# Batch 2's transposes moved to DMA, one in-place ring, and a new front order in a fused attention and FFN kernel

## The chip, the cores and the metric

One core of one Trainium2 chip. Kernels are compared only within the same rounds. The metric is device time in microseconds (us) of one execution. Single executions of one kernel differ by up to 3 us, so a profile (one execution) is used to say *where* time goes, and ratios over several runs say *how much*.

## The reference

```python
# q, k, v: (8 batches, 12 heads, 448 positions, 64)
scores = scale * np.matmul(q, k.transpose(0, 1, 3, 2))
attn = np.maximum(scores, 0.0) ** 2 / S
x = np.matmul(attn, v)                 # -> (3584 tokens, 768)
h = x @ w_in                           # 768 -> 2048
g = 0.5 * h * (1.0 + erf(h / sqrt(2))) # exact GELU
out = g @ w_out                        # 2048 -> 768
```

## The kernel before

Python builds the whole instruction order with a small list scheduler: every piece of work is an `Op` with estimated times, and each engine takes the ready op with the smallest key. The chip runs that fixed order. For batches from 2 on, TensorE's order is given: "slots" of attention with "atoms" of FFN mixed in. Below, QK is the product of q and k, AV that of the squared scores and v, and xT the AV result, which two copies bring from PSUM to SBUF. The first weights are `w_in`, the second weights `w_out`, and second products the matmuls with them. An FFN group is 6 matmuls 448 wide, or 12 of 224. Eviction is the work of VectorE and ScalarE that empties PSUM.

```python
WINDOW = 60                  # only the first 60 open ops of an engine are looked at
def pick(self, ops):
    ...
        key = (est + op.bias + (0.5 * dur if len(op.engines) > 1 else 0), n)
```

Transposes of q and k: batches 0 to 2 on TensorE with a PSUM copy, batches 3 to 7 by a VectorE permute and a DMA transpose on SP. `add_gate` makes GpSimd, which issues the loads, wait for the q transposes before its next load.

```python
def add_tk(b, g):            # TensorE
    ...                      # 14 nc.tensor.transpose into one PSUM tile "tp"
    op = sch.add((("PE", 0.45, 0.67),), fn, ld_k[b, g], need=("f",), mode="T", bias=T_BIAS)
    ev = sch.add(e_copy(2 * S, 2), fn2, [op] + old_T(b), frees=("f",))

def add_T_dma(b, after):     # SP: 3 of kT, then 4 of qT
    ...
        nc.sync.dma_start_transpose(get_T(b)[1][:, g]..., get_p()[1][:, g])

# attention: score -> relu (ACT, early also DVE) -> square (DVE) -> AV
box["ar"] = apool.tile([128, 2, S], BF16, tag="ar", name="a_relu")         # ring of 3
box["a2"] = apool.tile([128, 2, S], BF16, tag="a2", name="a_sq", bufs=NA)  # ring of 11
...
# order of the loads on GpSimd and of the early work
add_v(0, 0, 1)
for g in (1, 2):
    add_k(0, g, g + 1); add_q(0, g, g + 1, 0, HC); add_v(0, g, g + 1)
add_win(0); add_q(0, 0, G, HC, NC); add_win(1)
...                          # transposes and steps of batch 0, loads of batch 1 and 2
add_wout(0); add_wout(1)     # second weights, straight after batch 2's loads
add_steps(steps(1), dve=True)
for g in range(G):
    add_tk(2, g); add_tq(2, g)
...
    if b == 2:
        stage.append(x1[:8] + mix(x1[8:], x2))   # x1: FFN-in of batch 1, x2: FFN-out of batch 0
```

Of the kernel before, what the change touches and what calls it, by code (L numbers as in the profile page):

```python
# [9 lines left out]
BF16 = mybir.dt.bfloat16  # L10
# [6 lines left out]
HS = S // 2  # L17
KB = 64
NK = S // KB
NA = 11  # L20
HP = H // 2
G = H // 4
DM = H * D
# [3 lines left out]
ND = DM // 2  # L27
NB = 512
WINS = (2, 2, 4, 4, 4)
T_BIAS, AV_BIAS, F1_BIAS, GELU_BIAS = -0.3, 0.0, 0.2, -0.4  # L30


def cols(half):
# [7 lines left out]
class Op:  # L41
# [1 line left out]



    def __init__(self, engines, fn, deps=(), need=(), frees=(), bias=0.0, mode=None, joint=()):
        self.engines, self.fn, self.deps = engines, fn, list(deps)
        self.need, self.frees, self.bias, self.mode = need, frees, bias, mode
        self.joint = joint
        self.done = None  # L50


class Scheduler:



    SWITCH = 0.09
    COLD = 18.0
    WINDOW = 60

    def __init__(self, buffers):
        self.free = {"PE": 0.6, "ACT": 2.2, "DVE": 1.0, "POOL": 1.25, "SP": 0.9}
        self.bufs = {name: [0.0] * n for name, n in buffers.items()}
        self.open, self.mode, self.dma = [], None, 2.6
        self.landed = [0.0] * 8
        self.log = []

# [18 lines left out]
    def pick(self, ops):  # L86
        top = None
        for n, op in enumerate(ops):
            t = self.ready(op)
            if t is None:  # L90
                continue
            for eng, dur, lat in op.engines:
                est = max(t, self.free[eng])
                if isinstance(lat, tuple):
                    est = max(est, self.landed[-8])
                if eng == "PE" and op.mode != self.mode:
                    est += self.SWITCH
                key = (est + op.bias + (0.5 * dur if len(op.engines) > 1 else 0), n)
                if top is None or key < top[0]:
                    top = (key, est, op, eng, dur, lat)  # L100
        return top

    def commit(self, est, op, eng, dur, lat):
        if eng == "PE":
            self.mode = op.mode
            if est < self.COLD:
                dur, lat = 2 * dur, 2 * lat
        if isinstance(lat, tuple):
            t = max(self.dma, est + dur + 1.0)
            self.dma = t + lat[0] / (300e3 if t < 10 else 390e3)  # L110
            op.done = self.dma + 1.2
            self.landed += [op.done] * lat[1]
        else:
            op.done = est + lat
        self.free[eng] = est + dur
        for name in op.need:
            b = self.bufs[name]
            b[b.index(min(b))] = math.inf
        ends = [op.done] + [o.done for o in op.joint]
        if None not in ends:  # L120
            for name in op.frees:
                b = self.bufs[name]
                b[b.index(math.inf)] = max(ends)
        self.log.append((est, op, eng))
# [32 lines left out]
def kernel(  # L157
# [23 lines left out]
    tpool = pool("tpool", 2)  # L181
    xpool = pool("xpool", 2)
    hpool = pool("hpool", 2)
    apool = pool("apool", 3)
    opool = pool("opool", 3)
    w_pp = pool("w_pp", 3, PS)
    f_pp = pool("f_pp", 2, PS)
# [77 lines left out]
        d = 0.07 + n / psum / 960  # L265
        return ("DVE", d, d + 0.12), ("ACT", 0.12 + 0.00074 * n, 0.24 + 0.00074 * n)

    sch = Scheduler({"w": 3, "ar": 3, "a2": NA, "f": 2, "osb": 3})
    pool_q, pe_q = [], []

    def dma(fn, nbytes, deps=(), issues=1):
# [70 lines left out]
        for e in range(2):  # L342
            copy(dst[e], src[:, 2 * e : 2 * e + 2].rearrange("p j (c d) -> p j c d", d=D))  # L343

    def add_pk(b, g0, g1, after=()):
        for g in range(g0, g1):
            deps = ld_k[b, g] + [Tk[max(b - 1, 1), x][0] for x in range(G)] + list(after)
            Pk[b, g] = sch.add(
                (("DVE", 0.31, 0.43),),
                lambda e, g=g: permute_k(V.tensor_copy, g, nk[b][:, 2 * g : 2 * g + 2]), deps,  # L350
            )

    def add_pq(b, g0, g1, c0=0, c1=NC, after=()):
        for g in range(g0, g1):
            deps = [ld_q[b, g, c] for c in range(c0, c1)] + list(after)
            deps += [Tq[max(b - 1, 1), g, c][0] for c in range(c0, c1)]
            if b == 3:
                deps += [Tq[1, x, c][0] for x in range(G) for c in range(NC)]
            d = 2 * (0.07 + (c1 - c0) * 128 / 3840)

            def fn(e, g=g):
                permute_q(
                    V.tensor_copy, g, c0, c1, nq[b][:, 4 * g : 4 * g + 4, c0 * D : c1 * D]
                )

            op = sch.add((("DVE", d, d + 0.12),), fn, deps)
            for c in range(c0, c1):
                Pq[b, g, c] = op

    def old_T(b):  # L370
        return [o for (bb, *_), o in QK.items() if bb == b - 2]

    def add_tk(b, g):
        box = []

        def fn(e):
            tp = f_pp.tile([128, NK * 128], BF16, tag="f", name="tp")
            box.append(tp)
            for i in range(NK):
                for e in range(2):  # L380
                    nc.tensor.transpose(  # L381
                        tp[64 * e : 64 * e + 64, bass.ts(i, 128)],
                        nk[b][:, 2 * g + e, bass.ts(i, D)],
                        ident,
                    )

        def fn2(e):
            copy(e, get_T(b)[1][:, g], box[0])

        op = sch.add(  # L390
            (("PE", 0.45, 0.67),), fn, ld_k[b, g], need=("f",), mode="T", bias=T_BIAS
        )
        ev = sch.add(e_copy(2 * S, 2), fn2, [op] + old_T(b), frees=("f",))
        Tk[b, g] = (op, ev)
        return op

    def add_tq(b, g, c0=0, c1=NC):
        box, n = [], (c1 - c0) * KC

        def fn(e):  # L400
# [11 lines left out]
        def fn2(e):  # L412
            copy(e, get_T(b)[0][:, 2 * g : 2 * g + 2, c0 * KC : c1 * KC], box[0])

        d = 0.125 * (c1 - c0)
        deps = [ld_q[b, g, c] for c in range(c0, c1)]
        op = sch.add(
            (("PE", d, d + 0.22),), fn, deps, need=("f",), mode="T", bias=T_BIAS
        )
        ev = sch.add(e_copy(2 * n, 2), fn2, [op] + old_T(b), frees=("f",))  # L420
        for c in range(c0, c1):
            Tq[b, g, c] = (op, ev)
        return op
# [38 lines left out]
    def add_steps(todo, bias=0.0, dve=False):  # L462
        for blocks in todo:
# [17 lines left out]
                            )  # L481

            def fn_relu(e_, box=box, used=used):
                box["ar"] = apool.tile([128, 2, S], BF16, tag="ar", name="a_relu")
                ar, ps = box["ar"][:, :, :used], box["ps"][:, :, :used]
                if e_ == "ACT":
                    A.activation(ar, ps, AF.Relu, scale=c_att)  # L487
                else:
                    V.tensor_scalar(  # L489
                        ar, ps, c_att, 0.0,  # L490
                        op0=mybir.AluOpType.mult, op1=mybir.AluOpType.max,
                    )

            def fn_mul(e_, box=box, used=used):
                box["a2"] = apool.tile([128, 2, S], BF16, tag="a2", name="a_sq", bufs=NA)
                ar = box["ar"][:, :, :used]
                V.tensor_mul(box["a2"][:, :, :used], ar, ar)  # L497

            deps = []
# [7 lines left out]
            if dve:  # L507
                d = 0.07 + 2 * used / 960
                eng += (("DVE", d, d + 0.12),)
            o2 = sch.add(eng, fn_relu, [o1], need=("ar",), frees=("w",))  # L510
            d = 0.07 + used / 960
            o3 = sch.add((("DVE", d, d + 0.12),), fn_mul, [o2], need=("a2",), frees=("ar",))
            for x, blk in enumerate(blocks):
                QK[blk] = o1
                SQ[blk] = (o3, box, x * w)
# [4 lines left out]
    def add_av(blk, bias):  # L520
# [5 lines left out]
        def fn(e_):  # L526
# [19 lines left out]
        d = 7 * 0.19 * w / S  # L546
        op = sch.add(
            (("PE", d, d + 0.24),), fn, deps, mode="A", bias=bias + AV_BIAS, need=("w",),
            frees=("a2",) * gone,
        )  # L550
        AV[b, g, half] = op

# [7 lines left out]
        for j in range(2):  # L560
            xs.append(
                sch.add(
                    e_copy(w, 1), lambda e, j=j: copy(e, get_x()[:, j], pav[0][:, j, :w]),
                    [op] + old, frees=("w",), joint=list(xs),
                )
            )
        xs[0].joint = [xs[1]]
# [157 lines left out]
    ctx.enter_context(tc.manual_schedule())  # L725


    add_v(0, 0, 1)
    for g in (1, 2):
        add_k(0, g, g + 1)  # L730
        add_q(0, g, g + 1, 0, HC)
        add_v(0, g, g + 1)
    add_win(0)
    add_q(0, 0, G, HC, NC)
    add_win(1)
# [22 lines left out]
        add_tk(0, g)  # L758
        add_tq(0, g, 0, HC)
    for g in range(G):  # L760
        add_tq(0, g, HC, NC)
    add_steps(halves(0), dve=True)
    add_load(1, 0, 1)
    add_win(2)
    add_load(1, 1, 2)
# [1 line left out]
    add_load(1, 2, 3)  # L767
    add_win(4)
    for g in range(G):
        add_tk(1, g)  # L770
        add_tq(1, g)
    for m in range(0, KF, 2):
        add_f1(0, m, 0, bias=F1_BIAS)
    for g in range(G):
        add_load(2, g, g + 1)
    add_wout(0)
    add_wout(1)
    add_steps(steps(1), dve=True)
    for g in range(G):
        add_tk(2, g)  # L780
        add_tq(2, g)
    for m in range(0, KF, 2):
        add_f1(0, m, 1, bias=F1_BIAS)


    todo = [x for b in range(2, B) for x in steps(b)]
# [19 lines left out]
    for b in range(2, B):  # L806
        add_steps(steps(b))
        if b + 1 < B:

            n = per * (b - 2) + {2: 4, 3: 3}.get(b, 1)  # L810
            add_pk(b + 1, 0, G, after=at(n))
            add_pq(b + 1, 0, G, after=at(n))
            add_T_dma(b + 1, [at(n + (y >= 4)) for y in range(7)])
# [2 lines left out]
                add_load(b + 2)  # L816
        x1, x2 = f1(b - 1), f2(b - 2)
        if b == 2:
            stage.append(x1[:8] + mix(x1[8:], x2))
        else:  # L820
            stage.append(x2[:2] + mix(x1, x2[2:]))
    for n, slot in enumerate(order):
        for kind, x in slot:
            pe_q.append(AV[x] if kind == "AV" else QK[x])
# [39 lines left out]
```

## Time and profile before

| | before |
|---|---|
| median of 4 runs | 404.26 us (403.62 to 404.96) |
| span of the profiled run | 401.4 us, granted clock 0.996 |
| TensorE from first transpose to first FFN matmul ("front") | 6.14 to 24.64 us |
| from there to the first QK of batch 2 ("middle") | 24.64 to 64.25 us |
| from there on ("body") | 332 us, idle 0.36 us |

The lines behind the table are in the prediction. The page's shares say "TensorE, 97%", but that is an average: the body has one limit, and the front and middle have several (rows arriving, eviction of scores, order). A gain has to be looked for ahead of 64 us.

### The profile page before, as it was taken

To read this page: it belongs to the slowest core of one execution; us is meant where nothing else is said; L and a number is where in the kernel's file an instruction comes from. 1 tells how busy PE (TensorE), PEld (TensorE's weight loads), DVE (VectorE), ACT (ScalarE), POOL (GpSimd) and SP (SyncE) were. 2 spreads that over 40 slices of the span, in tenths; PEclk is the share of its full clock that TensorE was granted. 3 is DMA by queue.
4 is the path that set the end of the run, shared out by engine and by line. 5 is a ranking of instruction groups with operands and counts; after the bars stand their busy time and mean duration, and the time that the engine had idled before them with its cause. 6 is when DMAs were issued, how large, how long until landed. Compare 5 with 4: busy or idle time off the path is not lost.

```text
span 401.4 us, 8294 instructions
## 1 busy us (share of the span) xinstructions
PE 387.8 (97%) x3587; PEld 218.7 (54%) x3587; DVE 175.4 (44%) x323; ACT 214.8 (54%) x326; POOL 45.1 (11%) x67
## 2 busy tenths in 40 slices
PE   7699999999999999999999999999999999999995
PEld 6476686555555455555554555555555555555562
DVE  2989951454535434633373443634343433110111
ACT  2887956755746646656645565457645646222200
POOL 8755420000200200020001100000000000000000
PEclk9899999999999999999999999999999999999999
DMA  9999999719975592689137921470102011100132
GB/s 172 192 204 203 201 211 206 111 48 162 169 126 109 93 214 50 126 120 179 41 65 153 179 67 42 88 129 1 41 13 66 3 41 40 41 17 24 39 80 78
DMA packets 63750, 41.59 MB, mean 104 GB/s; under 512 B 32097, under 2 KB 60129, under 8 KB 63713
## 3 DMA queue, kind: packets, MB, share of 16 engines
q0 software_dynamic: 30496, 22.47, 37.3%
q1 hardware_dynamic: 32944, 18.13, 20.1%
q8 instruction: 28, 0.46, 0.5%
q10 hardware_dynamic: 272, 0.46, 0.3%
q14 instruction: 10, 0.07, 0.1%
HBM read 45.61 MB, written 11.01 MB: 141 GB/s over the span
## 4 chain that ended last, share of the span: by engine, by line
PE 86%; DVE 6%; DMA 3%; issue 2%; POOL 1%; ACT 0%; POOLq 0%
PE pso L621 36%; PE psh L581 36%; PE pav L534 7%; PE ps L475 7%; DVE a_sq L497 2%; DVE a_relu L489 2%; DMA nk<-in_k_dram 2%; DMA win_sb<-in_moe_w_in_dram 2%; POOL v_sb L307 1%; POOL nq L208 0%; DVE pq L343 0%; POOL nk L292 0%; PE tp L381 0%; DVE kT L259 0%; DVE osb L259 0%
## 5 line engine op out<-in xcount | busy, mean ns | idle before, releaser
L487 ACT ACTIVATE a_relu<-ps 128x896 bf16<-128x896 f32 (+1 forms) x156 | 136.9, 918 | 47.0 <-PE ps L475 45.1
L581 PE MATMUL psh<-xT,win_sb 128*128 128x448 bf16 (+1 forms) x864 | 156.2, 332 | 0.5 <-DVE osb L259 0.4
L621 PE MATMUL pso<-wout_sb,h_sb 128*128 128x384 bf16 x896 | 152.8, 326 | 0.0
L497 DVE TENSOR_TENSOR a_sq<-a_relu 128x896 bf16<-128x896 bf16 (+1 forms) x169 | 102.9, 620 | 81.8 <-ACT a_relu L487 81.8
L621 PEld LDWEIGHTS <-h_sb 128*128 128x128 bf16 x896 | 86.3, 98 | 63.1 <-issue 5.9
L581 PEld LDWEIGHTS <-win_sb 128*128 128x128 bf16 x864 | 80.9, 98 | 68.1 <-issue 13.6
L593 ACT ACTIVATE h_sb<-psh 128x448 bf16<-128x448 f32 x128 | 70.6, 552 | 76.4 <-PE psh L581 76.4
L259 DVE COPY osb<-pso 128x384 f32<-128x384 f32 x56 | 31.1, 556 | 92.7 <-PE pso L621 92.7
L475 PE MATMUL ps<-qT,kT 64*64 64x448 bf16 (+1 forms) x756 | 47.0, 340 | 2.8 <-DVE xT L259 1.4
L534 PE MATMUL pav<-a_sq,v_sb 64*64 64x448 bf16 (+1 forms) x756 | 37.4, 332 | 0.4 <-ACT a_relu L487 0.4
L261 ACT CAST xT<-pav 128x448 bf16<-128x448 f32 (+1 forms) x31 | 14.6, 482 | 33.8 <-PE pav L534 33.8
L475 PEld LDWEIGHTS <-kT 64*64 64x64 bf16 x756 | 19.2, 107 | 21.8 <-issue 15.5
L259 DVE CAST xT<-pav 128x448 bf16<-128x448 f32 (+1 forms) x23 | 13.7, 594 | 39.2 <-ACT xT L261 39.2
L534 PEld LDWEIGHTS <-v_sb 64*64 64x64 bf16 x756 | 19.7, 106 | 15.3 <-issue 7.4
L450 POOL COPY gate<-qT 128x4 bf16<-128x4 bf16 x4 | 0.8, 189 | 154.7 <-DMA qT<-pq 154.7
L489 DVE TENSOR_SCALAR a_relu<-ps 128x896 bf16<-128x896 f32 x13 | 14.1, 1082 | 0.5 <-PE ps L475 0.5
L208 POOL DMA_DIRECT2D nq<-in_q_dram x14 | 11.8, 840 | 2.6 <-PE ps L475 0.9
L307 POOL DMA_DIRECT2D v_sb<-in_v_dram x14 | 10.6, 760 | 2.9 <-DMA win_sb<-in_moe_w_in_dram 1.5
L292 POOL DMA_DIRECT2D nk<-in_k_dram x13 | 9.9, 764 | 8.8 <-PE ps L475 6.0
L381 PE MATMUL tp<-ident,nk 128*64 128x128 bf16 x126 | 5.6, 232 | 2.2 <-DMA nk<-in_k_dram 2.2
L406 PE MATMUL tp<-ident,nq 112*64 112x112 bf16 x144 | 5.9, 223 | 1.8 <-DMA nq<-in_q_dram 1.3
L343 DVE COPY pq<-nq 112x512 bf16<-112x512 bf16 x30 | 6.9, 285 | 0.0
(25 smaller groups left out, 51.9 us busy)
## 6 DMA issues: line engine op xcount, KB each, us to landing
nk<-in_k_dram POOLq DMA_DIRECT2D x5, 672.0 KB, 7.1
nq<-in_q_dram POOLq DMA_DIRECT2D x5, 672.0 KB, 10.7
v_sb<-in_v_dram POOLq DMA_DIRECT2D x5, 672.0 KB, 13.6
wout_sb<-in_moe_w_out_dram POOLq DMA_DIRECT2D x2, 1536.0 KB, 18.4
out_dram<-osb SPq DMA_DIRECT2D x8, 336.0 KB, 2.8
out_dram<-osb SPq DMA_DIRECT2D x8, 288.0 KB, 2.9
v_sb<-in_v_dram POOLq DMA_DIRECT2D x9, 224.0 KB, 8.4
out_dram<-osb SPq DMA_DIRECT2D x8, 240.0 KB, 2.7
```

The lines of the kernel that those rows point to most:

```text
L208: nc.gpsimd.dma_start(nq[b][:, 4 * g0 : 4 * g1, c0 * D : c1 * D], q_view(b, g0, g1, c0, c1))
L259: V.tensor_copy(dst, src)
L261: A.copy(dst, src)
L307: nc.gpsimd.dma_start(vt[b][:, 2 * g0 : 2 * g1], kv_view(v, b, g0, g1))
L475: nc.tensor.matmul(ps[64 * j : 64 * j + 64, e, x * w : x * w + w], kT[r, g, i * 128 + 64 * j : i * 128 + 64 * j + 64], qT[r, 2 * g + j, co ...
L487: A.activation(ar, ps, AF.Relu, scale=c_att)
L489: V.tensor_scalar(ar, ps, c_att, 0.0, op0=mybir.AluOpType.mult, op1=mybir.AluOpType.max,)
L497: V.tensor_mul(box["a2"][:, :, :used], ar, ar)
L534: nc.tensor.matmul(pav[0][o2 : o2 + 64, e, :w], vt[b][r, 2 * g + e, bass.ts(i, D)], box["a2"][r, e, o : o + w], start=(i == 0), stop=(i == ...
L581: nc.tensor.matmul(ph[:, x * n : x * n + n], win_sb[:, kd, bass.ts(m + x, 128)], xT[b][:, kd, c], start=(kd == 0), stop=(kd == KD - 1),)
L593: A.activation(hT[b // 2][:, m : m + nm, o + c.start : o + c.stop], box[0][:, :S].rearrange("p (x n) -> p x n", x=nm), AF.Gelu,)
L621: nc.tensor.matmul(po[:, :ND], hT[pr][:, kf, bass.ts(t, 128)], wout_sb[:, kf, bass.ts(n, ND)], start=(kf == 0), stop=(kf == KF - 1),)
```

## The change

Its intent: take batch 2's transposes off TensorE; put them ahead of the second weights in the load queue, so that the two don't run side by side; let relu and square share one ring; and place work of batch 0's first half in front. The diff, cut to its core, with some lines joined:

```diff
-NA = 11
+NA = 14
+T_BIAS, T_LATE, T_ONE, T_TWO = -0.5, 0.2, -0.16, 0.6    # and eight more biases
+DMA_FREE, DMA_LAT, LEAD = 4.0, 2.13, 5
 ...
-                key = (est + op.bias + (0.5 * dur if len(op.engines) > 1 else 0), n)
+                key = (est + op.bias + x * op.other, n)
 ...
-                box["ar"] = apool.tile([128, 2, S], BF16, tag="ar", name="a_relu")
+                box["a2"] = apool.tile([128, 2, S], BF16, tag="a", name="a_sq")
 ...                                        # the square writes the tile that it reads
-    add_v(0, 0, 1)
     for g in (1, 2):
         add_k(0, g, g + 1)
         add_q(0, g, g + 1, 0, HC)
-        add_v(0, g, g + 1)
+        add_v(0, g - 1, g)
+    add_v(0, 2, 3)
 ...
+        half = [order_only(QK[0, G - 1, NK - 1, 0])]
+        add_tk(1, g, T_ONE, half)          # batch 1's transposes after half 0's scores
+        add_tq(1, g, bias=T_ONE, after=half)
 ...
-    add_wout(0)
-    add_wout(1)
-    add_steps(steps(1), dve=True)
-    for g in range(G):
-        add_tk(2, g)
-        add_tq(2, g)
+    add_steps(steps(1), ATT1_BIAS, True)
+    for g in range(G):
+        add_pk(2, g, g + 1, bias=T_TWO)
+        add_pq(2, g, g + 1, bias=T_TWO)
+    add_T_dma(2, [[]] * 7)
+    add_gate(2)
+    add_wout(0)
+    add_wout(1)
 ...
-            n = per * (b - 2) + {2: 4, 3: 3}.get(b, 1)
+            n = per * (b - 2) + {2: 5, 3: 3}.get(b, 1)
 ...
-            stage.append(x1[:8] + mix(x1[8:], x2))
+            first_atoms = x1[:LEAD]        # ahead of batch 2's first scores
+            stage.append(x1[LEAD:] + x2)
```

More of the change, by code (lines that the diff above doesn't have):

```diff
@@ L29 @@
 WINS = (2, 2, 4, 4, 4)
-T_BIAS, AV_BIAS, F1_BIAS, GELU_BIAS = -0.3, 0.0, 0.2, -0.4
+T_BIAS = -0.5
+T_LATE = 0.2
+T_ONE = -0.16
+T_TWO = 0.6
+AV_BIAS = -0.11
+X_BIAS = -0.2
+F1_BIAS = 0.2
+F1B_BIAS = 0.2
+ATT1_BIAS = 0.0
+HALF_BIAS = -0.07
+GELU_BIAS = -0.57
+RELU_DVE = 0.36
+DMA_FREE = 4.0
+DMA_LAT = 2.13
+SWITCH = 0.09
+LEAD = 5
 def cols(half):
@@ L41, with __init__, done @@
 class Op:
-    def __init__(self, engines, fn, deps=(), need=(), frees=(), bias=0.0, mode=None, joint=()):
+    def __init__(self, engines, fn, deps=(), need=(), frees=(), bias=0.0, mode=None, joint=(),
+                 other=0.0):
         self.engines, self.fn, self.deps = engines, fn, list(deps)
         self.need, self.frees, self.bias, self.mode = need, frees, bias, mode
+        self.other = other
         self.joint = joint
-        self.done = None
+        self.start = self.done = None
+class order_only:
+    def __init__(self, op):
+        self.op = op
+    @property
+    def done(self):
+        return self.op.start
 class Scheduler:
-    SWITCH = 0.09
     COLD = 18.0
@@ L63, in __init__ @@
         self.bufs = {name: [0.0] * n for name, n in buffers.items()}
-        self.open, self.mode, self.dma = [], None, 2.6
+        self.open, self.mode, self.dma = [], None, DMA_FREE
         self.landed = [0.0] * 8
@@ L91, in pick @@
                 continue
-            for eng, dur, lat in op.engines:
+            for x, (eng, dur, lat) in enumerate(op.engines):
                 est = max(t, self.free[eng])
@@ L96, in pick @@
                 if eng == "PE" and op.mode != self.mode:
-                    est += self.SWITCH
-                key = (est + op.bias + (0.5 * dur if len(op.engines) > 1 else 0), n)
+                    est += SWITCH
+                key = (est + op.bias + x * op.other, n)
                 if top is None or key < top[0]:
@@ L103, in commit @@
     def commit(self, est, op, eng, dur, lat):
+        op.start = est
         if eng == "PE":
@@ L109, in commit @@
             t = max(self.dma, est + dur + 1.0)
-            self.dma = t + lat[0] / (300e3 if t < 10 else 390e3)
-            op.done = self.dma + 1.2
+            self.dma = t + lat[0] / 390e3
+            op.done = self.dma + DMA_LAT
             self.landed += [op.done] * lat[1]
@@ L183 @@
     hpool = pool("hpool", 2)
-    apool = pool("apool", 3)
+    apool = pool("apool", NA)
     opool = pool("opool", 3)
@@ L266, in e_copy @@
         return ("DVE", d, d + 0.12), ("ACT", 0.12 + 0.00074 * n, 0.24 + 0.00074 * n)
-    sch = Scheduler({"w": 3, "ar": 3, "a2": NA, "f": 2, "osb": 3})
+    sch = Scheduler({"w": 3, "a": NA, "f": 2, "osb": 3})
     pool_q, pe_q = [], []
@@ L343, in permute_q, with add_pk @@
             copy(dst[e], src[:, 2 * e : 2 * e + 2].rearrange("p j (c d) -> p j c d", d=D))
-    def add_pk(b, g0, g1, after=()):
+    def add_pk(b, g0, g1, after=(), bias=0.0):
         for g in range(g0, g1):
@@ L350, in add_pk, with add_pq @@
                 lambda e, g=g: permute_k(V.tensor_copy, g, nk[b][:, 2 * g : 2 * g + 2]), deps,
+                bias=bias,
             )
-    def add_pq(b, g0, g1, c0=0, c1=NC, after=()):
+    def add_pq(b, g0, g1, c0=0, c1=NC, after=(), bias=0.0):
         for g in range(g0, g1):
@@ L356, in add_pq @@
             deps += [Tq[max(b - 1, 1), g, c][0] for c in range(c0, c1)]
-            if b == 3:
+            if b == 2:
                 deps += [Tq[1, x, c][0] for x in range(G) for c in range(NC)]
@@ L364, in fn @@
                 )
-            op = sch.add((("DVE", d, d + 0.12),), fn, deps)
+            op = sch.add((("DVE", d, d + 0.12),), fn, deps, bias=bias)
             for c in range(c0, c1):
@@ L371, in old_T, with add_tk @@
         return [o for (bb, *_), o in QK.items() if bb == b - 2]
-    def add_tk(b, g):
+    def add_tk(b, g, bias=T_BIAS, after=()):
         box = []
@@ L390, in add_tk, with add_tq @@
         op = sch.add(
-            (("PE", 0.45, 0.67),), fn, ld_k[b, g], need=("f",), mode="T", bias=T_BIAS
+            (("PE", 0.45, 0.67),), fn, ld_k[b, g] + list(after), need=("f",), mode="T", bias=bias
         )
-        ev = sch.add(e_copy(2 * S, 2), fn2, [op] + old_T(b), frees=("f",))
+        ev = sch.add(e_copy(2 * S, 2), fn2, [op] + old_T(b), frees=("f",), bias=bias)
         Tk[b, g] = (op, ev)
         return op
-    def add_tq(b, g, c0=0, c1=NC):
+    def add_tq(b, g, c0=0, c1=NC, bias=T_BIAS, after=()):
         box, n = [], (c1 - c0) * KC
@@ L415, in add_tq @@
         d = 0.125 * (c1 - c0)
-        deps = [ld_q[b, g, c] for c in range(c0, c1)]
+        deps = [ld_q[b, g, c] for c in range(c0, c1)] + list(after)
         op = sch.add(
-            (("PE", d, d + 0.22),), fn, deps, need=("f",), mode="T", bias=T_BIAS
+            (("PE", d, d + 0.22),), fn, deps, need=("f",), mode="T", bias=bias
         )
-        ev = sch.add(e_copy(2 * n, 2), fn2, [op] + old_T(b), frees=("f",))
+        ev = sch.add(e_copy(2 * n, 2), fn2, [op] + old_T(b), frees=("f",), bias=bias)
         for c in range(c0, c1):
@@ L483, in fn_relu @@
             def fn_relu(e_, box=box, used=used):
-                box["ar"] = apool.tile([128, 2, S], BF16, tag="ar", name="a_relu")
-                ar, ps = box["ar"][:, :, :used], box["ps"][:, :, :used]
+                box["a2"] = apool.tile([128, 2, S], BF16, tag="a", name="a_sq")
+                ar, ps = box["a2"][:, :, :used], box["ps"][:, :, :used]
                 if e_ == "ACT":
@@ L494, in fn_mul @@
             def fn_mul(e_, box=box, used=used):
-                box["a2"] = apool.tile([128, 2, S], BF16, tag="a2", name="a_sq", bufs=NA)
-                ar = box["ar"][:, :, :used]
+                ar = box["a2"][:, :, :used]
                 V.tensor_mul(box["a2"][:, :, :used], ar, ar)
@@ L509, in add_steps @@
                 eng += (("DVE", d, d + 0.12),)
-            o2 = sch.add(eng, fn_relu, [o1], need=("ar",), frees=("w",))
+            o2 = sch.add(
+                eng, fn_relu, [o1], need=("a",), frees=("w",), bias=bias, other=RELU_DVE
+            )
             d = 0.07 + used / 960
-            o3 = sch.add((("DVE", d, d + 0.12),), fn_mul, [o2], need=("a2",), frees=("ar",))
+            o3 = sch.add((("DVE", d, d + 0.12),), fn_mul, [o2], bias=bias)
             for x, blk in enumerate(blocks):
@@ L548, in add_av @@
             (("PE", d, d + 0.24),), fn, deps, mode="A", bias=bias + AV_BIAS, need=("w",),
-            frees=("a2",) * gone,
+            frees=("a",) * gone,
         )
@@ L563, in add_av @@
                     e_copy(w, 1), lambda e, j=j: copy(e, get_x()[:, j], pav[0][:, j, :w]),
-                    [op] + old, frees=("w",), joint=list(xs),
+                    [op] + old, frees=("w",), joint=list(xs), bias=bias + X_BIAS,
                 )
@@ L760 @@
     for g in range(G):
-        add_tq(0, g, HC, NC)
-    add_steps(halves(0), dve=True)
+        add_tq(0, g, HC, NC, T_LATE)
+    st0 = halves(0)
+    add_steps(st0[:11], dve=True)
+    add_steps(st0[11:], HALF_BIAS, True)
     add_load(1, 0, 1)
@@ L769 @@
     for g in range(G):
-        add_tk(1, g)
-        add_tq(1, g)
+        half = [order_only(QK[0, G - 1, NK - 1, 0])]
+        add_tk(1, g, T_ONE, half)
+        add_tq(1, g, bias=T_ONE, after=half)
     for m in range(0, KF, 2):
@@ L775 @@
         add_load(2, g, g + 1)
+    add_steps(steps(1), ATT1_BIAS, True)
[4 more added lines that the diff above has]
+    add_gate(2)
     add_wout(0)
     add_wout(1)
-    add_steps(steps(1), dve=True)
-    for g in range(G):
-        add_tk(2, g)
-        add_tq(2, g)
     for m in range(0, KF, 2):
-        add_f1(0, m, 1, bias=F1_BIAS)
+        add_f1(0, m, 1, bias=F1B_BIAS)
     todo = [x for b in range(2, B) for x in steps(b)]
@@ L818 @@
         if b == 2:
-            stage.append(x1[:8] + mix(x1[8:], x2))
+            first_atoms = x1[:LEAD]
+            stage.append(x1[LEAD:] + x2)
         else:
             stage.append(x2[:2] + mix(x1, x2[2:]))
+    pe_q.extend(x[1] for x in first_atoms)
     for n, slot in enumerate(order):
```

## The prediction

> **What bounds the kernel now.** I read the page first, then the busy time per stretch, then what TensorE waited for, then the timeline and the chain for the stretch that the change touches.
>
> The page's shares and its forty slices of 10 us (busy tenths):
>
> ```profile
> PE 387.8 (97%) x3587; PEld 218.7 (54%) x3587; DVE 175.4 (44%) x323; ACT 214.8 (54%) x326; POOL 45.1 (11%) x67
> ...
> PE   7699999999999999999999999999999999999995
> ...
> DVE  2989951454535434633373443634343433110111
> ACT  2887956755746646656645565457645646222200
> ...
> DMA  9999999719975592689137921470102011100132
> ```
>
> TensorE has gaps only in the first slices; VectorE and ScalarE are near full only in slices 2 to 5, and the DMA engines are full for the first seven. So the kernel has a start with several limits, and from about 52 us a body with one limit, TensorE. Busy time by stretch, cut where the first FFN matmul (24.64) and the first QK of batch 2 (64.25) stand in the timeline; columns are length, then PE, PEld, DVE, ACT, POOL busy, granted clock, DMA share, GB/s:
>
> ```profile
> 6.14:24.64 18.50, 13.13 (x336) 9.60 (x337) 14.80 (x27) 12.69 (x19) 13.49 (x20) 0.91 1.40 194
> 24.64:64.25 39.61, 38.02 (x637) 29.67 (x634) 30.41 (x49) 29.63 (x47) 15.54 (x21) 1.00 1.25 206
> ...
> 64.25:396.50 332.25, 331.89 (x2577) 174.83 (x2576) 128.82 (x243) 170.41 (x258) 11.07 (x16) 1.00 0.46 86
> ```
>
> From 64.25 to 396.5 TensorE idles 0.36 us in 332. Nothing in the change removes TensorE work there, so all the gain must lie ahead of 64.25.
>
> Busy time hides short losses, so I price the work ahead of 64.25 at the rates of the chain, from one start to the next: QK 0.70 us for 24 half-width or 0.69 for 12 full-width matmuls; AV 0.80 for 28 half-width, 1.45 full-width; 14 k transposes 0.51, 16 q transposes 0.52; first FFN product 7.01 for 72. Counts are from the timeline.
> - 6.14 to 24.64: 132 QK = 3.8, 3 AV = 2.4, 4 k groups = 2.0, 4 q groups = 2.1. Sum 10.3 of 18.5: 8.2 lost.
> - 24.64 to 64.25: 36 half and 84 full QK = 5.9, 3 half and 3 full AV = 6.75, 5 k and 5 q groups = 5.15, 192 FFN matmuls = 18.7. Sum 36.5 of 39.6: 3.1 lost.
>
> So 46.8 us of work takes 58.1 us; the most that better order can ever win is 11.3. What TensorE waited for between 5 and 25 us:
>
> ```profile
> PE tp L381 <- DMA nk<-in_k_dram: 2.2, 2, 1.1
> PE tp L406 <- DMA nq<-in_q_dram: 1.1, 1, 1.1
> PE ps L475 <- ACT a_relu L487: 1.1, 3, 0.4
> PE ps L475 <- DVE xT L259: 0.9, 2, 0.6
> PE tp L406 <- ACT nq L261: 0.4, 1, 0.4
> ```
>
> 5.7 us of named waits: 3.3 stand in front of transposes whose rows had not landed while other work lay behind them in order; 2.0 are full score buffers. [...]
>
> [...]
>
> **The change part by part.**
>
> 1. Batch 2's transposes leave TensorE. They are these six groups:
>
> ```profile
> 42.96 0.58 PE L381 MATMUL tp<-ident,nk 128*64 128x128 bf16 x14
> ...
> 44.33 0.58 PE L406 MATMUL tp<-ident,nq 112*64 112x112 bf16 x16
> ...
> 46.41 0.58 PE L381 MATMUL tp<-ident,nk 128*64 128x128 bf16 x14
> ...
> 47.43 0.58 PE L406 MATMUL tp<-ident,nq 112*64 112x112 bf16 x16
> ```
>
> and two more at 50.01 and 51.49. 3 x 0.51 + 3 x 0.52 = 3.1 us off TensorE, in a stretch where it loses almost nothing else: about all of it reaches the end. Six PSUM copies go too, 3 on VectorE (0.54 each) and 3 on ScalarE (0.9): 4.3 us. VectorE gains 3 permutes of k (384 ns) and 6 of q (285 ns): 2.9 us. Net the two engines lose 1.4 us of 87.5 (the two stretches' DVE plus ACT): small, and beside other work.
>
> 2. The transposes on SP. From the groups and the DMA issues:
>
> ```profile
> L343 DVE COPY pq<-nq 112x512 bf16<-112x512 bf16 x30 | 6.9, 285 | 0.0
> ...
> wout_sb<-in_moe_w_out_dram POOLq DMA_DIRECT2D x2, 1536.0 KB, 18.4
> ...
> qT<-pq SPq DMA_TRANSPOSE x20, 2.7
> kT<-pk SPq DMA_TRANSPOSE x15, 3.1
> ```
>
> Batch 2's last k and q loads are issued at 40.9 and 42.0 and take about 8.6: landed by 50.6. Permutes to 51.5; four q transposes at 1.3 each on SP (4 took 5.39 at 92.65) plus the landing: done near 58, 60 if VectorE is late. The new order puts the rest of batch 0's FFN and five groups of batch 1's (5 x 1.15 = 5.75) ahead of the first QK of batch 2: 58 + 5.8 = 64. Margin 4 us or more: hidden.
>
> 3. The second weights behind the gate. 3.1 MB at 0.207 MB/us is 15 us[...]: there at 76 to 78 instead of 66. First use moves from 75.4 to: all 16 FFN groups of batch 1 (18.4), ten QK steps (2.3), an AV and switches (1.9) after 58, about 80.6. Hidden by 3 to 5 us. This is why the order of that stage changed.
>
> 4. The front. q and k of groups 1 and 2 move ahead of v by one 224 KB load, 1.1 us at 0.2 MB/us; late q transposes and batch 1's transposes are held back, so TensorE should not stand in front of unlanded rows. Of the 3.3 us of such waits I expect 2.0 to go; the rest only turns into waits for eviction, since VectorE and ScalarE are at 25.8 of 30 engine-us between 10 and 25 us. First-half priority brings the first FFN groups forward, but only the four tiles of the first two weight loads have landed before about 26 us (two groups, 2.4 us of filler): 0.8.
>
> 5. One ring of 14 in place of 3 and 11: same bytes, same instructions. It removes the waits of ScalarE's relu for VectorE's square (1.8 us, 5 times), off TensorE's path mostly: 0.4.
>
> Sum: 3.1 + 2.0 + 0.8 + 0.4 = 6.3. 404.7 - 6.3 = 398.4.
>
> **Rivals.**
> - Eviction takes over: with transposes gone, TensorE's early stretch is paced by relu and square. For it: VectorE busy 9.98 of 10 between 40 and 50 us, and the permutes are all VectorE. Against it: VectorE's last square of batch 1 ends at 54.8 and TensorE has 10 us of ready FFN work after that. Then 3.1 plus little: 401.
> - The DMA chain is late: transposes slowed beside saturated loads (DMA full until 76 us), QK of batch 2 or the second weights wait. Each us late beyond the margin of 3 to 5 costs a us. For it: no transpose of the old kernel ran beside full loads. Against: the gate leaves the q transposes almost alone. 400 to 404.
> - The reorder does far more than I credit: most of the 8.2 lost early goes. For it: the waits are of order, not of work. Against: bytes and eviction still pace it. 395 to 396.
> - A slower square in place: 0.1 us on each of 167 would fill VectorE, but in the body it is at 39%; +0 to +2.
>
> **Range and chances.** Low end: 3.1 plus half of the 11.3 lost, 8.8: 395.9. High end: only the 3.1 less a stall, or none: 402. 2% is 8.1 us, which needs 5.0 of the 11.3 beside the transposes; I give it 0.22. Slower by 2% needs a stall of over 14 us: 0.03.
>
> **What would show it.** Groups: 84 k and 96 q transposes on TensorE instead of 126 and 144, and 18 and 24 DMA transposes. First QK of batch 2 near 64, with no TensorE wait on qT or kT; first FFN product of batch 1 near 58 instead of 64.8; first second-product near 80, no wait on the second weights; TensorE's waits for nk and nq under 1.5 us; squares still near 620 ns. From there 332 us of work less the five moved groups, as before. The prediction is wrong if TensorE idles over a microsecond anywhere after 58, if the early waits merely change their names, or if the body's rate changes.

That busy time hides losses is shown in the front: 13.13 us are counted busy there, for 10.3 us of work at the rates of the chain. The sum of the forecast's five parts has all its terms: 6.3 us, so 398.4. Part 3 got to "76 to 78" with a further 3 us, the estimate for issuing the second weights and for landing, with no trace named for it; without it the 15 us alone give 73 to 75. In the changed kernel 19.1 us passed from the first issue (64.57) to the last landing (83.7). The "switches" in part 3 are changes of TensorE between one kind of matmul and another: in the timeline of the kernel before, an FFN group of 6 took 1.23 us up to the start of an AV (78.03 to 79.26) and 1.13 up to that of a second product (83.70 to 84.83). What makes up the 2.5 us of the 8.2 that the named waits leave is not shown.

## The result, and the profile after

| | before | after |
|---|---|---|
| median | 404.26 us (4 runs) | 400.50 us (398.98 to 400.81, 4 runs) |
| ratio | | 0.9899 (0.9867 to 0.9931) |
| the same again in other rounds (expected: 400 to 400.8) | 404.20 us (11 runs) | 399.01 us (5 runs), ratio 0.9879 (0.9861 to 0.9898) |
| span of the profiled run | 401.4 us | 398.9 us; 397.2 us in the repeat |

So 4.1 to 4.9 us came off (1.0 and 1.2% of 404.2). I had said 6.3. The page of the changed kernel, same rows as before:

```profile
PE 385.3 (97%) x3497; PEld 215.8 (54%) x3497; DVE 173.1 (43%) x329; ACT 213.3 (53%) x323; POOL 45.2 (11%) x68
...
PEclk9879999999999999999999999999999999999998
DMA  9999966999895891897148921560111011110122
```

TensorE has 90 matmuls fewer, as planned. The DMA row has a dip in slices 6 and 7 (50 to 70 us): the gate holds the second weights back there, to 64.6 us. Busy time of the three stretches, cut at the same events (columns as in the prediction):

```profile
6.08:25.50 19.42, 13.93 (x336) 10.42 (x337) 13.78 (x25) 13.18 (x20) 13.41 (x20) 0.82 1.38 194
25.50:65.82 40.32, 40.16 (x572) 29.49 (x571) 29.22 (x55) 31.09 (x49) 12.62 (x19) 1.00 1.01 159
65.82:394.00 328.18, 327.05 (x2547) 171.96 (x2546) 128.74 (x244) 166.91 (x252) 14.19 (x20) 1.00 0.53 96
```

- **Front:** 19.42 us where it was 18.50. It got longer, at a granted clock of 0.82.
- **Middle:** 40.32 us, but it now holds five FFN groups of batch 1 (30 matmuls, 5.7 us), so 34.6 us for what took 39.6. This is the whole gain: 5.0 us, of which the prediction's price of the transposes would make 3.1.
- **Body:** TensorE idles 1.1 us where it idled 0.36.

What TensorE waited for, in the whole run after:

```profile
PE tp L410 <- DMA nk<-in_k_dram: 2.1, 2, 1.5
PE ps L504 <- ACT a_sq L516: 1.6, 5, 0.5
PE tp L435 <- DMA nq<-in_q_dram: 1.3, 1, 1.3
...
PE ps L504 <- DMA qT<-pq: 0.4, 1, 0.4
```

The waits for nk and nq are 3.4 us; they were 3.5. The new one is for qT of batch 3 at 104.34 us, 0.4 us.

**The front differs from run to run.** The repeat ran the same program. Its first five-microsecond stretches, first the profile of the changed kernel, then that of the repeat:

```profile
15.00:20.00 5.00, 2.89 (x68) 2.17 (x67) 3.42 (x6) 3.65 (x7) 4.37 (x7) 0.77 1.47 195
20.00:25.00 5.00, 4.17 (x90) 3.47 (x90) 2.48 (x6) 2.42 (x4) 2.38 (x4) 0.55 1.26 205
```

```profile
15.00:20.00 5.00, 2.15 (x68) 1.58 (x67) 3.27 (x6) 3.92 (x7) 4.53 (x7) 1.00 1.47 195
20.00:25.00 5.00, 4.42 (x114) 3.57 (x118) 3.80 (x8) 3.84 (x5) 2.25 (x5) 1.00 1.26 205
```

The ninth number is the granted clock: 0.77 and 0.55 in the one, 1.00 in the other. TensorE gets 90 matmuls done in the second stretch in place of 114. The first FFN matmul is at 25.50 and 23.66 us, the spans are 398.9 and 397.2. The middle is equal to 0.01 us (40.32 and 40.31). Most of the 1.8 us can be read off: after the wait for batch 1's first k rows, which ends at 20.83 and 20.58, the same work up to the first FFN matmul takes 4.67 us in the one and 3.08 in the other, so 1.6 us go with the low clock and 0.25 with rows that came later. The kernel before had a dip too, 0.88 and 0.78, but between 5 and 15 us.

**The second weights arrive just in time.** First the SP queue and then the GpSimd queue of the changed kernel (start, length):

```profile
53.10 4.46 SPq L459 DMA_TRANSPOSE kT<-pk  x3
57.66 5.21 SPq L467 DMA_TRANSPOSE qT<-pq  x4
```

```profile
64.34 0.18 POOL L479 COPY gate<-qT 128x4 bf16<-128x4 bf16 x1 [21.06 <-DMA qT<-pq]
64.57 1.78 POOL L259 DMA_DIRECT2D wout_sb<-in_moe_w_out_dram  x2
```

Two loads start at 64.6 and 65.5 and take 11.6 and 18.2 us: landed at 76.2 and 83.7. The first second product begins at 82.35 and needs the second half of the weights 1.3 us later, at 83.7. The margin is nil.

### The profile page after: what moved, and what is told of

Its sections match the earlier page's. It is cut to its first block, busy times and chain, and to the rows that moved or that the text cites. A ratio compares the mean times of both kernels' runs of the same rounds, so it can differ in the third digit from the quotient of the medians.

```text
span 398.9 us, 8136 instructions
## 1 busy us (share of the span) xinstructions
PE 385.3 (97%) x3497; PEld 215.8 (54%) x3497; DVE 173.1 (43%) x329; ACT 213.3 (53%) x323; POOL 45.2 (11%) x68
## 4 chain that ended last, share of the span: by engine, by line
PE 86%; DMA 4%; ACT 3%; DVE 2%; SPq 1%; POOL 1%; issue 1%; POOLq 0%; DVEq 0%; ACTq 0%
PE psh L611 36%; PE pso L651 35%; PE ps L504 8%; PE pav L564 7%; ACT a_sq L516 2%; DMA win_sb<-in_moe_w_in_dram 2%; DMA nk<-in_k_dram 2%; SPq L467 1%; DMA qT<-pq 1%; POOL v_sb L335 1%; DVE xT L287 0%; DVE a_sq L525 0%; DVE osb L287 0%; POOL nk L320 0%; PE tp L410 0%
## 5 line engine op out<-in xcount | busy, mean ns | idle before, releaser
L516 ACT ACTIVATE a_sq<-ps 128x896 bf16<-128x896 f32 (+1 forms) x161 | 140.7, 920 | 35.7 <-PE ps L504 35.7
L525 DVE TENSOR_TENSOR a_sq<-a_sq 128x896 bf16<-128x896 bf16 (+1 forms) x169 | 103.0, 621 | 104.9 <-ACT a_sq L516 104.8
L289 ACT CAST xT<-pav 128x448 bf16<-128x448 f32 (+1 forms) x26 | 12.9, 496 | 48.7 <-DVE xT L287 47.8
L287 DVE CAST xT<-pav 128x448 bf16<-128x448 f32 (+1 forms) x28 | 15.8, 566 | 29.7 <-PE pav L564 29.3
L236 POOL DMA_DIRECT2D nq<-in_q_dram x14 | 11.6, 827 | 1.5 <-DMA win_sb<-in_moe_w_in_dram 0.6
L518 DVE TENSOR_SCALAR a_sq<-ps 128x896 bf16<-128x896 f32 x8 | 8.6, 1085 | 0.7 <-PE ps L504 0.7
L371 DVE COPY pq<-nq 112x512 bf16<-112x512 bf16 x36 | 8.3, 287 | 0.3 <-DMA nq<-in_q_dram 0.3
L435 PE MATMUL tp<-ident,nq 112*64 112x112 bf16 x96 | 4.2, 230 | 2.3 <-DMA nq<-in_q_dram 1.3
L360 DVE COPY pk<-nk 128x896 bf16<-128x896 bf16 x18 | 6.1, 386 | 0.0
```

What stands on the lines that cost most here:

```text
L236: nc.gpsimd.dma_start(nq[b][:, 4 * g0 : 4 * g1, c0 * D : c1 * D], q_view(b, g0, g1, c0, c1))
L287: V.tensor_copy(dst, src)
L289: A.copy(dst, src)
L516: A.activation(ar, ps, AF.Relu, scale=c_att)
L525: V.tensor_mul(box["a2"][:, :, :used], ar, ar)
```

## The experiments

Medians and ratios are against the kernel before in the same rounds. "Front + middle" is from the first transpose to the first QK of batch 2, less 5.7 us where the five groups stand in it; "body" is from the first 32 second products in a row after 100 us to the last block of 128. Both are from one profile each, so the first carries the luck of its front (54.0 and 52.1 for one program); the second does not.

| kernel | median us | ratio | front + middle | body |
|---|---|---|---|---|
| before | 404.26 | | 58.1 | 267.34 |
| after | 400.50 | 0.9899 | 54.0 | 268.26 |
| after, repeated | 399.01 | 0.9879 | 52.1 | 268.24 |
| e1: transposes back on TensorE | 402.57 | 0.9967 | 55.8 | 268.25 |
| e2: before + DMA transposes only | 401.21 | 0.9928 | 54.0 | 267.34 |
| d1: e2 + one ring | 401.38 | 0.9937 | 55.4 | 267.35 |
| e7: after with two rings | 401.55 | 0.9951 | 54.4 | 268.20 |
| e3: after, old tie rule late | 398.81 | 0.9867 | 52.1 | 267.34 |

### e1 and e2: is it the transposes or the order?

e1 puts batch 2's transposes back on TensorE in the changed kernel:

```diff
-        add_pk(2, g, g + 1, bias=T_TWO)
-        add_pq(2, g, g + 1, bias=T_TWO)
-    add_T_dma(2, [[]] * 7)
-    add_gate(2)
+        add_tk(2, g, T_ONE)
+        add_tq(2, g, bias=T_ONE)      # and the second weights ahead, ungated
```

> The changed kernel with batch 2's transposes back on TensorE and the second weights ungated; everything else of the change stays. Theory (the transposes off TensorE are worth their 3.1 us, the rest of the change about nothing net): about 3.1 us slower than the changed kernel, 403 to 404. Rival (the new order gives the gain, and the transposes were beside other work): 400 to 401.5. Trace: 126 and 144 transposes on TensorE.

e2 moves only those transposes, in the kernel before:

```diff
-    for g in range(G):
-        add_tk(2, g)
-        add_tq(2, g)
+    add_pk(2, ...), add_pq(2, ...), add_T_dma(2, [[]] * 7), add_gate(2)   # then add_wout
 ...                        # and five FFN groups of batch 1 ahead, as in the change
```

> The kernel before with only batch 2's transposes moved to DMA, the gate ahead of the second weights, and the order of that stage that goes with them; its own front, rings and tie rule stay. Theory: 404.3 - 3.1 = 401.2, a little better if the body keeps the old rate (401). Rival (the new order gives the gain): 403.5 to 404.5. If late permutes or transposes stop TensorE, over 402 with a named wait on kT or qT.

Measured: e1 402.57 us, ratio 0.9967; e2 401.21 us, ratio 0.9928 (0.9915 to 0.9941). Moving the transposes alone is worth 2.9 us of 404. Leaving them out of the change costs 0.9967 - 0.9879 = 0.88% or 0.9967 - 0.9899 = 0.68% (the two measurements of the changed kernel): 2.7 to 3.6 us. Both sides agree with 3.1, and the rival falls. e1's own median, 402.57, came out half a microsecond under what I had written: in these runs the rest of the change is worth 1.3 us (0.6 to 2.1) and not nothing.

### e3: where does the body lose 0.9 us?

```diff
-                key = (est + op.bias + x * op.other, n)
+                key = (est + op.bias + x * op.other
+                       + (0.5 * dur if len(op.engines) > 1 and est > 62 else 0), n)
```

> The changed kernel with the old tie rule for two-engine copies from 62 us of its own plan on, so that the first of the two xT copies after each AV goes to ScalarE again. Theory (the body loses 1.0 us because relu waits on ScalarE behind a second, later xT copy): 0.7 to 1.1 us faster than the changed kernel, 399.5, with steps of the chain between 105 and 395 us as in the kernel before. Rival (those 1.0 us come from somewhere else in the body): 400.5, unchanged.

Measured: 398.81 us, ratio 0.9867 (0.9852 to 0.9882); body 267.34 us, exactly that of the kernel before. The body is so even that one profile settles it: all seven kernels with the old rule in the body (before, e2, d1, e3 and the later c0, c1, c2) have 267.34 or 267.35, all seven profiles with the new rule 268.20 to 268.26. What the rule does shows at one AV, first in the kernel before, then in the changed one (timeline of that place):

```profile
175.26 0.53 ACT L261 CAST xT<-pav 128x448 bf16<-128x448 f32 x1 [3.52 <-PE pav L534]
175.69 0.92 ACT L487 ACTIVATE a_relu<-ps 128x896 bf16<-128x896 f32 x1
175.83 0.62 DVE L259 CAST xT<-pav 128x448 bf16<-128x448 f32 x1 [1.47 <-ACT xT L261]
```

```profile
171.87 0.62 DVE L287 CAST xT<-pav 128x448 bf16<-128x448 f32 x1 [0.90 <-PE pav L564]
172.58 0.53 ACT L289 CAST xT<-pav 128x448 bf16<-128x448 f32 x1 [4.12 <-DVE xT L287]
173.01 0.93 ACT L516 ACTIVATE a_sq<-ps 128x896 bf16<-128x896 f32 x1
...
175.23 0.38 PE L504 MATMUL ps<-qT,kT 64*64 64x448 bf16 x4 [0.16 <-ACT a_sq L516]
```

The two copies of an AV result run one after the other in both kernels. With the old rule ScalarE copies first (its relu begins 0.43 us after its copy). With the new one VectorE comes first, ScalarE idles until 172.58, and the relu behind it starts 1.14 us after the first copy and not 0.43. A score buffer comes free later and TensorE waits, here 0.16 us. After 100 us the profile names only 0.3 us of such waits, so how the rest of the 0.92 is spread is not shown; that the rule costs it is shown by e3. The old `0.5 * dur` term had broken the tie for ScalarE; nobody meant to change that.

### e4: does the slow clock set the front?

```diff
+            if (b, g, c0) == (0, 0, HC):
+                busy(24)      # matmuls of zeros into a spare PSUM tile
 ...
+            if (b, g) == (1, 0):
+                busy(28)
```

> The changed kernel with 24 and 28 matmuls of zeros placed ahead of the two transposes that stand waiting for rows near 15.5 and 19.5 us. Theory (those two waits bring the granted clock down to about half between 17.5 and 24 us, and the work after them runs slow): granted clock near 1.0 there, first FFN matmul 1 to 2 us earlier than 25.5, time 398.5 to 399.5. Rival (the low clock only falls into waiting, which rows and eviction set anyway): clock up, first FFN matmul still at 25 to 25.5, time 400 to 401.

Measured: 399.64 us, ratio 0.9894 (0.988 to 0.9909). The granted clock between 15 and 25 us is 1.00, and the mean clock of its five runs is 0.997 to 1.0 where the changed kernel's nine runs have 0.988 to 0.996. The first FFN matmul comes at 24.28, 1.2 us earlier than in the changed kernel's dipped profile. But 0.8 us of that is taken back: TensorE now waits that long for the second weights. So neither text held: the granted clock was 1.00 and the front faster, and the time is not better than the changed kernel's (0.9879 and 0.9899). The repeat of the changed kernel had no dip without any zeros (its k rows also landed 0.6 us sooner than e4's).

The dip itself is no exception. Of the fourteen profiles nine show a granted clock under 0.8 in some five microseconds between 10 and 25 us; of the five without one, four are kernels whose early waits for rows were filled or shortened (e4, and e5, c0, c2 below), and the fifth is the repeat. In the changed kernel's profile the clock was 0.50 between 19 and 23 us. That waits bring it down was the theory, and these runs do not settle it: the repeat waited 3.8 us for nk and nq without a dip, e6 1.9 us with one (0.62). But where the dip was nearly over by 20 us, the first FFN matmul shows no cost: e3 (0.72, then 0.93) and c1 (0.66, then 1.00), with the same front, have it at 23.62 and 23.55 us, as early as the repeat. Where it lasted from 20 to 25 us, 0.55 in the changed kernel and 0.70 in e6, that matmul came at 25.50 and 24.45. So where the dip falls differs from run to run, it is worth up to about 1.6 us, and preventing it this way does not pay.

### e5: rows ahead of the first weights

```diff
     add_v(0, 2, 3)
-    add_win(0)
     add_q(0, 0, G, HC, NC)
+    add_k(1, 0, 1)
+    add_q(1, 0, 1)
+    add_win(0)
     add_win(1)
+    add_v(1, 0, 1)
```

> The changed kernel with the second half of batch 0's q and the first k and q of batch 1 loaded ahead of the first two pieces of the first weights. Theory (the front waits for rows, and what it gains is then taken back because the second weights land at a time that the transposes set): the two waits for nq and nk near 16 and 20 us go (3.4 us to under 1), first FFN matmul 1.5 to 3 us earlier than 25.5, but the second products then wait 1 to 2 us for the second weights; time 399 to 400.2. Rival (nothing binds after the front): the 2 us reach the end, 398 to 398.7. Rival (eviction or the first weights bind the front): first FFN matmul at 24.5 to 25.5, time 400 to 401.

Measured: 399.35 us, ratio 0.9886, beside 0.9879 of the repeat: no gain. The waits for nk and nq fell from 3.8 us (repeat) to 1.7, the first FFN matmul moved from 23.66 to 22.80, the second products waited 0.75 us:

```profile
80.73 1.46 PE L651 MATMUL pso<-wout_sb,h_sb 128*128 128x384 bf16 x8
82.94 1.46 PE L651 MATMUL pso<-wout_sb,h_sb 128*128 128x384 bf16 x8 [0.75 <-DMA wout_sb<-in_moe_w_out_dram]
```

My theory was half right. The second weights do cap the end (0.75 us; the repeat waits 0.4). But most of the front's gain was gone before that: the first QK of batch 2 stands at 64.20, in the repeat at 63.97. TensorE's waits for ScalarE's and VectorE's xT copies (1.2 us in all, none in the repeat) took their place. So, as the named waits read, the early stretch stays bounded by eviction even with earlier rows, the rival that I had named in another form.

### e6: is the gate worth it?

```diff
-    add_gate(2)
     add_wout(0)
     add_wout(1)
+    add_gate(2)
```

> The changed kernel with the second weights issued straight after batch 2's loads, ahead of the gate, so that they move beside batch 2's transposes. Theory (the gate costs nothing here because the second weights just make it, and the transposes need quiet DMA engines): transposes land later than 64.3, by 2 to 6 us, the first QK of batch 2 waits for qT by about as much less 1.5, time 401 to 405. Rival (transposes beside full loads are hardly slower): transposes done by 65, second weights at 67, no wait for either; 400 to 400.5.

Measured: 410.50 us, ratio 1.0162 (1.0144 to 1.018): 11 us slower than the changed kernel. The SP queue, and then TensorE at the first QK of batch 2:

```profile
52.05 13.80 SPq L459 DMA_TRANSPOSE kT<-pk  x3
65.95 6.83 SPq L467 DMA_TRANSPOSE qT<-pq  x4
```

```profile
74.23 0.96 PE L504 MATMUL ps<-qT,kT 64*64 64x448 bf16 x8 [9.39 <-DMA qT<-pq]
```

Three k transposes hold SP for 13.8 us where they took 4.46 behind the gate, and TensorE stands 9.39 us. The direction of the theory held, but not its size: 401 to 405 us was written. The rival falls. Only the place of the gate was changed, so it is the load of the second weights that slows the transposes; in what way was not looked into. "Ahead of the second weights" is not a detail of the change but its condition.

### e7 and d1: what is the ring worth?

e7 gives the changed kernel its two rings of 3 and 11 back; d1 gives e2 the one ring of 14.

```diff
-                box["a2"] = apool.tile([128, 2, S], BF16, tag="a", name="a_sq")
+                box["ar"] = apool.tile([128, 2, S], BF16, tag="ar", name="a_relu")
 ...
+                box["a2"] = apool.tile([128, 2, S], BF16, tag="a2", name="a_sq", bufs=11)
```

> The changed kernel with the relu in a ring of 3 and the square in one of 11 again. Theory (the one ring is worth 0.4 us or less, and the square in place costs nothing): 400.3 to 401, squares at 620 ns in both. Rival (the one ring carries the better stretch from 25 to 60 us): 401.5 to 402.5, with ScalarE's relu waiting for VectorE's square again.

> e2 with one ring of 14 added: the kernel before with batch 2's transposes by DMA and relu and square in place in one ring, but with its own front order, biases and tie rule. Theory (the changed kernel's new front is worth about nothing net, its tie rule costs 0.9 us in the body, and the ring is worth 1.5 to 2.9 us as e7 showed from the other side): e2's 401.2 less 1 to 2 us, about 399 to 400, as good as the changed kernel. Rival (the ring only pays together with the new front): 400.8 to 401.5, as e2. Rival (the new front is worth 1 us or more): 400.2 to 401, with the ring worth under 1 us here.

Measured: e7 401.55 us, ratio 0.9951, against 0.9879 of the repeat: the ring is worth 2.9 us in the changed kernel (2.1 against the first measurement, 0.9899). The rival's number held, its mechanism not, as the end of this part says. d1 401.38 us, ratio 0.9937 (0.9921 to 0.9952), against e2's 0.9928: it is worth nothing in the old order, and the rival that it only pays with the new front held. And e7 itself, the new order without the ring, is 0.9 us *slower* than e2 (the two intervals overlap), about what its tie rule loses in the body: the new order alone brings nothing that these runs show. Neither half pays alone; the pair does, most clearly in e3, which is 2.5 us under e2 (0.9867 and 0.9928). TensorE between 30 and 40 us, first in e7, then in the repeat of the changed kernel:

```profile
30.00:40.00 10.00, 9.24 (x148) 6.32 (x145) 9.39 (x15) 9.53 (x16) 4.85 (x7) 1.00 1.27 203
```

```profile
30.00:40.00 10.00, 9.86 (x162) 7.15 (x166) 9.56 (x18) 9.31 (x15) 5.19 (x9) 1.00 1.27 204
```

162 matmuls in the same 10 us in place of 148. In d1 the first FFN matmul is at 27.20 us, later than in e2 (25.00): TensorE waits 1.4 us for ScalarE ahead of two AV products near 25 us. A plausible reading is that a long ring lets the plan put relus of later blocks ahead of those that an AV is waiting for, and the new biases hold them back; I did not test it further. The square itself is as fast in place: 621 ns mean against 620. The named wait of relu for square, on which I had built my 0.4 us, does not appear between 9 and 60 us in e7, and d1, which takes that wait out of the old order, is no faster for it. So that was not the mechanism.

### c0, c1, c2: can a version beat both?

The permutes of batch 2 ran late. Two things in the plan can hold them back: they are added to the list after batch 1's steps, perhaps beyond the 60 ops that `pick` looks at, and they have a bias of 0.6. c1 adds them ahead, with bias 0, on top of e3, and so does not tell which of the two it was; c0 is e3 and e5 together; c2 is all three.

```diff
+    (permutes and DMA transposes of batch 2, T_TWO = 0.0)
     add_steps(steps(1), ATT1_BIAS, True)
-    (permutes and DMA transposes of batch 2, T_TWO = 0.6)
     add_gate(2)
```

> e5 and e3 together: rows ahead of the first weights, and the old tie rule from 62 us on. Theory (the second weights, whose time the transposes set, cap what the front can win; the body's 0.9 us is separate): the body from the first group of 32 second products on as in e3, about 267.3 us to the last group; TensorE waits 0.8 to 1.5 us for the second weights; time 398.2 to 398.8. Rival (no such cap): 397 to 397.7 without that wait.

> e3 with batch 2's permutes planned ahead of batch 1's steps, so that VectorE does them as the rows land and not after batch 1's squares. Theory (late permutes made the gate late): gate opens near 60 instead of 63 to 64, second weights land near 79, TensorE's wait for them gone; time as e3 less that wait, 398.3 to 398.8, since the front is as it was. Rival (k transposes then run beside batch 2's loads and are slowed as in e6): gate at 63 or later, no change.

> c0 and c1 together. Theory: with the gate earlier the front's gain is no longer taken back: no wait for the second weights, first group of 32 second products of the next stage 1 us or more earlier than in c0; time 397 to 397.8, faster than both kernels of the case. Rival (eviction sets the stretch from 25 to 60 us, and the permutes there cost VectorE what they save): 398.3 to 399.

| | median us | ratio | gate opens | wait for second weights |
|---|---|---|---|---|
| c0 | 398.71 | 0.9872 (0.9854 to 0.9891) | 63.3 | 0.7 |
| c1 | 398.47 | 0.9868 (0.9847 to 0.9889) | 60.5 | none |
| c2 | 397.87 | 0.9851 (0.9833 to 0.9869) | 59.7 | none |

In c2 the SP queue reads:

```profile
43.94 8.63 SPq L459 DMA_TRANSPOSE kT<-pk  x3
52.67 5.51 SPq L467 DMA_TRANSPOSE qT<-pq  x4
```

The k transposes are spread over 8.63 us, as the permutes run at 43.47, 46.78 and 50.24 us between other work, but they start 9 us earlier, and the gate opens at 59.7 and not 64.3. c0 and c1 came out at the times of their theories, c0 with a wait of 0.7 us where 0.8 to 1.5 was written; c1 alone is not told apart from e3. c2 missed its 397 to 397.8 by a little, and its first 32 second products in a row came 0.65 us earlier than in c0 (102.88 and 103.53), not 1. It is 0.8 us under c0, about the wait that it removes, though the two intervals overlap. By its median it is the fastest kernel: 6.0 us (0.9851) under the kernel before, and 1.1 to 1.9 under the changed one (0.9879 and 0.9899; the intervals still touch, so that it beats the changed kernel is likely and not shown).

## Why the prediction was right or wrong

The time (400.5, again 399.0) lies in the range 395.9 to 402.0 and "within 2%" was given 0.75. The middle, 398.4, was 0.6 to 2.1 us too low; it started from 404.7, where the median of the kernel before came to 404.26, so the forecast change of 6.3 was 1.4 to 2.2 too large. That it came as near is partly luck: a term of 2.8 us that failed and a loss of 0.9 that was not foreseen were offset by a ring worth far more than its 0.4. By its own signs it failed at three: the waits for nk and nq stayed over 1.5 us, the repeat waits 0.4 us for the second weights, and the body's rate changed. Its steps:

- **Transposes off TensorE, 3.1 us: right.** e2 2.9 us alone, e1 2.7 to 3.6 from the other side.
- **The transposes on SP, done near 58, 60 if late: 4 to 6 us too early, hidden all the same.** The gate opened at 64.3 (62.8 in the repeat). I had the permutes done at 51.5, as soon as rows had landed; they ran from 52.6 to 56.6, behind batch 1's squares. And I counted the four q transposes but not the three of k ahead of them in the same queue (4.46 us). First QK of batch 2: 65.82 and 63.97, no wait for kT or qT, as predicted; but its margin was about 1.5 us in the profiled run, not 4.
- **The second weights, margin 3 to 5 us: wrong, nil.** It follows from the step above. They landed at 83.7 and were needed at 83.7. In the repeat TensorE waits 0.4 us, in e4 and e5 0.8. The rival "the DMA chain is late" named this; its size was small because the late chain and the later use nearly met.
- **The front, 2.0 + 0.8 us: wrong.** The waits for nk and nq were to shrink by 2.0; they stand at 3.4, from 3.5. Holding the transposes back did not help, because in the fixed order they are still the next work when TensorE runs idle, and the change hardly moves the loads of those rows (issued at 8.96 and 13.28 us before, at 8.69 and 13.97 after): the two transposes start at 16.82 and 20.12 us before, at 16.85 and 20.83 after, each straight from its wait. e5, which moves those loads, brings the waits down to 1.7 us. Whether ready work stood behind the transposes, as the prediction says, was not read from any trace. "First-half priority brings the first FFN groups forward": 23.66 us in the repeat against 24.64, so 1.0 at best, and 25.50 in the run with the slow clock. I had read the granted clock of 0.91 in the front of the kernel before and never asked what it could do: it goes with 1.6 of the 1.8 us by which the fronts of two runs of one program differ.
- **The ring, 0.4 us: wrong in size and in mechanism.** It is worth 2.9 us (2.1 by the first measurement), but only with the new order (e7, d1). I priced a named wait that d1 shows to be worth nothing; how the ring acts with the new order stays open.
- **The body, "as before": wrong by 0.92 us.** The prediction doesn't mention the changed key at all. e3 shows that it decides which engine makes the first of the two xT copies all through the body (at each of 16 AVs from 100 us on: VectorE in the changed kernel, ScalarE in e3).

In sum, by these runs: 3.1 for the transposes, 2.9 for the ring with the order that it needs, nothing for the front by itself, 0.9 taken back in the body and 0.4 in waits for qT or the second weights: 4.7, where 4.1 to 4.9 was measured. This is no independent check, since the parts come from the same measurements as the whole. The 2.8 of the front was the term that failed, and the ring's 0.4 the one that was mis-sized the other way. What stays open is how the ring and the biases work on each other between 25 and 60 us: the runs show that they only pay together, not why.

## What to carry to other kernels

When work leaves a saturated engine, its own price is easy and held here within the error (3.1 us predicted, 2.7 to 3.6 measured); the orders that it shifts are what needs pricing, down to every step of a serial queue (permutes, three transposes, four transposes, gate, load). In a kernel with a planned order, a changed tie rule or buffer count is a change of the plan everywhere, so compare a stretch that "isn't touched" to the tenth of a microsecond: an even body of 267.34 us gave the cause of a 0.9 us loss away in one profile. And before a profile is read for what moved, look at the granted clock of the stretch: two runs of one program, 0.55 and 1.00 between 20 and 25 us, differed there by 1.6 us, more than the tie rule's 0.9.
